# Segment 3 of a gated attention and long-convolution kernel: attention's two parts added on VectorE before the transpose, in a new order of steps

## The chip, the core and the metric

The kernel runs on one core of a Trainium2 chip. The metric is the device time of one execution in microseconds; lower is better. TensorE (PE; its weight loads are shown apart as PEld), VectorE (DVE), ScalarE (ACT), GpSimd (POOL) and SyncE (SP) run their own instruction streams in order and wait for each other by semaphores. DMAs are issued from the queues of SP and ACT here.

## What is computed

Two branches read the same x, 2048 rows of 512, and a gate mixes them by row:

```python
g = sigmoid((x * gate_w).sum(-1, keepdims=True))
out = g * A(x) + (1 - g) * B(x)
```

A is attention with 32 heads of 16 in four segments of 512 rows, with a memory M, z of the segments before. Per head and segment:

```python
logits = qs @ ks.T * scale + mask
a_dot = softmax(logits) @ vs
pq = phi(qs)                      # phi(t) = t + 1 if t > 0 else exp(t)
a_mem = (pq @ M) / (pq @ z + 1e-6)
o = sig(beta) * a_mem + (1 - sig(beta)) * a_dot
M, z = M + phi(ks).T @ vs, z + phi(ks).sum(0)
```

The o of all heads side by side are multiplied by wo. B is a long convolution of x with a kernel made from state-space parameters; the program does it with two levels of transforms written as matmuls, and adds a skip term.

## The kernel before

The program is recorded first and replayed after. `build_graph` makes a list of 1678 steps; each step names its engine, a function that issues its instructions, and the tiles that it reads and writes. `ORDER` is a table of numbers, made ahead of time: each entry is a step's number, then, after a slash, the buffer that each new tile takes; a letter a or v says whether ACT or DVE does a step that either can do. `replay` (line 233) walks the table, and `emit` (line 262) gives each engine its steps in that order, with the waits that the data and the reuse of buffers need. So the order on every engine and on every DMA queue, the choice of engine for copies out of PSUM, and the buffers all come from this table.

Almost every matmul is issued by one helper, so PE's rows read line 707. `evac` (line 222) copies a PSUM tile to SBUF: line 224 on ACT or 225 on DVE, lines 227 and 228 with a scale.

Attention. Heads are taken in four groups of eight (hg 0 to 3) per segment s. `project` makes q and k, `scores` does five score tiles per group: PE writes the scores into banks 0 to 3 of PSUM, ACT makes their exponential (line 1182, eighty in all), DVE masks them (line 1195), and PE multiplies them with v (the 17-column matmuls). `norm` divides by the sums (lines 1146, 1147, 1149) into `o1`, a bf16 tile of 128x512. `ophase` (line 1212) reads the memory for s > 0 (136-column matmuls; lines 1229, 1232 and 1233 on DVE) into `o2`, also bf16 128x512. It then brings both into the transposed form that the product with wo needs, as `oT`:

```python
        srcs = [o1] + ([o2] if o2 is not None and s < SUMO else [])
        one = len(srcs) == 1
        P3 = S.ps(dt=BF16 if one else F32)

        def f3(e):
            for tb in range(4):
                if one:
                    i = e.transpose(ap(P3, tb * 128, n=128), ap(o1, tb * 128, n=128), ap(ident, n=128))
                    continue
                for si, T in enumerate(srcs):
                    i = mm(e, ap(P3, tb * 128, n=128), ap(T, tb * 128, n=128), ap(ident, n=128), si == 0 and tb == 0, si == len(srcs) - 1)
```

With `SUMO = 4` no segment has the sum made on DVE (line 1237): in segments 1 to 3 PE multiplies o1 and o2 with the identity, eight matmuls of 128 columns that add up in a float32 PSUM tile. Segment 0 has no o2 and transposes o1 alone (four, line 1247).

The convolution. `ssm_prep`, `ssm_powers`, `ssm_cb` and `tables` make the transform of its kernel, mostly on DVE (lines 802 to 884 and 1286 to 1306). `x_level1` transforms x and writes it to scr_Z in HBM. `tail` runs twice (halves a and b): spectra (lines 1424 to 1433), products (1458), inverse transforms (1477).

The end. `early` multiplies the oT of segments 0 and 1 with wo (512-column matmuls, four to a tile) and puts the results back over oT. `finals` does the last level of the convolution (256-column matmuls with 32 rows of output, 16 to a tile) and adds attention: for segments 0 and 1 on DVE (line 1532), for 2 and 3 by more 512-column matmuls into the same PSUM tile, followed by the gate's scale (lines 227, 228, 1536, 1537). Segment 3's last tiles take three of their four head groups first and the fourth, hg 3, last. Output rows go out by DMA from SP and ACT.

The first loads: the identity comes by ACT's queue; the log of dt, x, the parameters, `c_W` (the first transform) and the weights by SP's.

Of the kernel before, what the change touches and what calls it, by code (L numbers as in the profile page):

```python
# [366 lines left out]
SUMO = 4  # L367
# [9 lines left out]
192/0 10/0 9/1 206/1 388/0 215/0 15/0 0/0 59/1 12/2 22/0 16/0 7/0 1210/0 27/3 3/0 28/0 17/0 20/0 25/1 33/0 13/1 26  # L377
42/12 23/0 60/7 35/0 43/1 34/6 36/2 1/0 41/11 62/4 37/3 38 39 1189/1 40 48/0 44/3 50/4 61v/0 14/4 49/5 1221/1 51/13
11/5 53/6 1211/0 63a 45 52 46 64/0 66/0 1213/4 47 1212a/0 1223/5 65 67v/4 76/0 211/2 78/5 1214a 79v/0 77 55/2 1215
90/2 88/2 19/0 91v/6 207/6 56/4 89 18/0 1224v/1 100/2 373/0 102/5 54/13 195/3 101 212a 103v/7 112/0 58/0 29/5 80 104  # L380
114/1 1197/7 31/0 113 81 57 1195/4 1190/2 92 188/0 68 1222a 30v/0 124/3 126/3 1225 209/1 189 1196a/0 181/4 69 1198a
1205/5 32v/1 213/4 208a 115v/1 1199 125 210a 1207/7 93 201/0 72/2 70/0 176/7 5/0 136/1 204/1 139v/2 105 138/6 202a/2
137 214a 1192/0 116 140 196/0 205a/0 127v/3 141 389/3 177/2 1206a/1 203/1 1208a 178/0 148/1 184/3 1218/1 223/0
151a/5 224 1191v/0 390a 150/5 293/2 225/1 149 965v/0 179/2 1193a 163v/8 226/0 182/1 227 197/0 294a/0 1194 383/0 185
1209 228/2 190 117 252/3 969/1 966v 164 128 180 129 384v/1 160/2 230/0 216 231 198 253a/1 71 1216/2 199/0 374/0
191/0 232/0 970 165 255/3 967v 162/9 579/0 971/0 84/7 972/0 1219a/0 295/2 238/0 375 968v 239 1217a 973 229/0 391/1
240/1 254/0 24 152 974/1 1228/2 217 233 200/0 977/0 1220 256a/2 975 242/0 234 392a 183 976 376 1229a/1 243 986/1
1226/1 244/0 1252/0 218/2 235/0 380/3 161 2/0 985 978 987 381a/2 264/0 219/0 979 265 1227a 241/3 220/0 245 988 266/0
1230 246 980/1 153 1202/1 82/3 981 271/0 4/0 272 1203a/0 172 247/2 989/1 173 273/1 395/1 83 236 983/0 94/1 248 982
267/0 268 396a 269/2 237/0 1200/1 296/2 990 1231/1 984 580/0 1201a 279/0 581 992/1 280 297a/0 1204 1265/1 270/0  # L390
281/0 274 382/1 275 186 96/3 1263/2 276/3 997 1264a/1 249 283/0 277 284 1266a 998/0 278/1 285/1 1267 999 257/1
1255/3 221 784/0 377 1001/0 222/2 1000 282/0 991 258/0 310/0 1256a/0 311 259/0 312/2 260 286 287 95 378 993 332/1
1253/3 106/3 288/0 303/0 1002 304 333a/1 107/1 994 305/0 1234/1 1235a/1 289 1003 306/0 290 307 1254a 1232/1 193 261
308/1 1257 995/1 298/3 250/0 1027/0 1233a 194 318/0 319 299/0 1236 262/0 309/1 320/0 313 301 335/2 300/0 108 996 314
118/1 322/0 120/6 323 336a/2 1004/1 324/1 315/4 1005 119 1010/3 316 1011 1012 263/0 1237/2 317/0 130/3 334/0 1014/4
1025/1 73v/7 1015 1238a/1 1006/7 132/4 1007 1016a/0 187 1008 582 74 1013a 785/5 1028/0 1023a/0 1247/1 1239/2 1026
1249/3 1009a 1021v 786 1024v 251a/0 1022v 344/0 1032 1248a/0 345 1033/0 1030/1 321/0 1240a 346/1 1034 1241 1244/2
1029 393/1 1250a 85v/0 1031 351/0 109a/4 1251 352 1036/0 325 394a 1035 353/2 440/1 1041 1242/3 1042/1 110 326 111
441a/0 86 347/0 1037 87 1243a/1 348 437/1 1043 349/1 1017/0 1038 327/2 1045/0 438a/0 363/0 1047 1245a 364 350/1
365/0 354 1246 337/3 328 1044 75 302/2 1039/1 355 338/0 397 359/0 1046 97a/1 360 329 1019 1053 361/1 485/0 339/0  # L400
1054/0 1040 291/3 292a 404/0 1055 121a/6 405 98 1057/1 340 486a/1 1056 341 406/0 1048/0 1270/0 1268/3 1271a/1 407/0
1058 408 1269a 342 1059 409/2 362/2 1272 1060/1 1260/0 1258/3 1049 366 367 99 1061 1259a/0 593/1 411/0 1020 1018
1051/0 412 1261a 413/1 1262 596/0 1050 600/3 122 1052 133a/2 399/4 601a 134 597a 131 1070/6 135 1062/7 356/1 400/0
# [1237 lines left out]
```

## Time and profile before

| | us |
|---|---|
| three runs | 282.5, 282.64, 284.19 (median 282.64) |
| the profiled execution | 282.45 |
| its span, first to last instruction | 280.6 |
| PE busy | 247.3 |
| DVE busy | 261.4 |
| ACT busy | 251.1 |

The span is what the trace shows of the profiled execution; the rest of its time lies around it. In the profile's groups a line gives the number of instructions, their busy time in all, the mean of one in ns, and the engine's idle time before them. Since an engine starts an instruction while the one before it drains, the busy time of a group is less than the count times the mean. In the chain and the timeline a row gives the start, the length, the engine and the line.

### The profile page before, as it was taken

The numbers are of one execution on the slowest core, as the hardware profiler recorded it, in microseconds if no ns is written. First come the engines' busy times: TensorE is split into PE (matmuls) and PEld (weight loads), VectorE is DVE, ScalarE is ACT, GpSimd is POOL, SyncE is SP. The second block draws the span as 40 slices with busy tenths as digits, with TensorE's granted clock in tenths as the row PEclk, the third lists the DMA queues.
The fourth block names the chain that finished last, engine by engine and source line by source line (L and its number), as shares of the span: only waits on it lengthen the run. The fifth ranks groups of instructions, "written<-read, shape, count | busy, mean of one in ns | idle before, by whom it ended". The sixth has DMA issues, their size and how long they took to land.

```text
span 280.6 us, 11488 instructions
## 1 busy us (share of the span) xinstructions
PE 247.3 (88%) x5042; PEld 160.0 (57%) x5042; DVE 261.4 (93%) x641; ACT 251.1 (89%) x310; POOL 5.1 (2%) x11
## 2 busy tenths in 40 slices
PE   2677887878978899999999998899999999999994
PEld 1342354645555766677666576566477656656672
DVE  0999999999999999999999999999999999998772
ACT  3999999999999999999999999999999998987621
POOL 5000000000000000000000000000000000000000
PEclk9999999999999999999999999999999999999999
DMA  7895493621232545334632646677577775330136
GB/s 171 261 247 139 126 221 98 183 65 41 88 89 61 160 111 174 116 94 105 223 103 70 176 134 199 198 216 245 160 248 195 232 210 154 86 97 5 40 92 172
DMA packets 47427, 40.70 MB, mean 145 GB/s; under 512 B 21265, under 2 KB 44818, under 8 KB 47378
## 3 DMA queue, kind: packets, MB, share of 16 engines
q1 hardware_dynamic: 46226, 39.43, 49.6%
q8 instruction: 39, 0.64, 1.0%
q10 hardware_dynamic: 1152, 0.56, 0.8%
q14 instruction: 10, 0.08, 0.1%
HBM read 20.64 MB, written 6.29 MB: 96 GB/s over the span
## 4 chain that ended last, share of the span: by engine, by line
PE 40%; ACT 35%; DVE 17%; issue 5%; DMA 1%; ACTq 0%
PE psum L707 40%; ACT sb L1182 19%; ACT sb L224 11%; DVE sb L225 3%; ACT sb L840 1%; DVE sb L1432 1%; DVE sb L848 1%; DVE sb L1195 1%; DMA sb<-c_ident 1%; DVE sb L847 1%; ACT sb L855 1%; DVE sb L1458 1%; DVE sb L856 1%; ACT sb L1022 1%; DVE sb L1292 1%
## 5 line engine op out<-in xcount | busy, mean ns | idle before, releaser
L707 PE MATMUL psum<-sb 128*64 128x17 bf16 (+16 forms) x4938 | 240.8, 222 | 24.2 <-ACT sb L1182 11.1
L707 PEld LDWEIGHTS psum<-sb 128*64 128x64 bf16 (+8 forms) x4938 | 153.5, 102 | 108.3 <-ACT sb L1182 23.7
L1182 ACT ACTIVATE sb<-psum 128x2048 bf16<-128x2048 f32 (+1 forms) x80 | 138.1, 1726 | 9.9 <-PE psum L707 9.2
L224 ACT ACTIVATE sb<-psum 128x512 bf16<-128x512 f32 (+6 forms) x151 | 91.7, 660 | 3.4 <-PE psum L707 3.0
L1289 DVE TENSOR_TENSOR sb<-sb 128x512 bf16<-128x512 bf16 (+2 forms) x44 | 30.5, 702 | 0.0
L1286 DVE TENSOR_TENSOR sb<-sb 128x512 bf16<-128x512 bf16 (+2 forms) x44 | 30.5, 701 | 0.0
L1292 DVE TENSOR_TENSOR sb<-sb 128x512 bf16<-128x512 bf16 (+2 forms) x44 | 30.3, 703 | 0.0
L1458 DVE TENSOR_TENSOR sb<-sb 128x1024 bf16<-128x1024 bf16 x32 | 21.1, 678 | 0.0
L225 DVE CAST sb<-psum 128x512 bf16<-128x512 f32 (+1 forms) x28 | 19.4, 702 | 0.5 <-PE psum L707 0.3
L1195 DVE TENSOR_TENSOR sb<-sb 128x512 bf16<-128x512 bf16 (+1 forms) x40 | 18.3, 468 | 0.0
L1432 DVE TENSOR_TENSOR sb<-psum,sb 128x512 bf16<-128x512 f32 x26 | 16.9, 680 | 0.5 <-ACT sb L224 0.4
L1149 DVE TENSOR_TENSOR sb<-psum,sb 128x256 bf16<-128x256 f32 x32 | 13.3, 415 | 0.2
L840 ACT ACTIVATE sb<-sb 128x512 f32<-128x512 f32 x18 | 11.7, 649 | 1.1 <-DVE sb L847 0.8
L1146 DVE RECIPROCAL sb<-psum 128x16 f32<-128x16 f32 x32 | 7.9, 247 | 1.1 <-PE psum L707 1.1
L1233 DVE TENSOR_TENSOR sb<-psum,sb 128x512 bf16<-128x512 f32 x12 | 8.2, 687 | 0.2
L1079 ACT ACTIVATE sb<-sb 128x512 bf16<-128x512 bf16 x12 | 7.6, 634 | 0.0
L1022 ACT ACTIVATE sb<-psum 128x512 bf16<-128x512 bf16 x12 | 7.4, 620 | 0.2 <-PE psum L1019 0.2
L848 DVE SCALAR_TENSOR_TENSOR sb<-sb 128x256 f32<-128x256 f32 (+1 forms) x18 | 7.4, 414 | 0.0
L847 DVE TENSOR_TENSOR sb<-sb 128x256 f32<-128x256 f32 (+1 forms) x18 | 7.4, 413 | 0.0
L1532 DVE SCALAR_TENSOR_TENSOR sb<-psum,sb 128x512 bf16<-128x512 f32 x8 | 5.9, 733 | 1.6 <-PE psum L707 1.6
L225 DVE COPY sb<-psum 128x512 f32<-128x512 f32 (+1 forms) x8 | 6.7, 837 | 0.2
L776 DVE COPY sb<-psum 128x512 bf16<-128x512 bf16 x1 | 0.7, 724 | 6.5 <-PE psum L773 6.5
(87 smaller groups left out, 123.2 us busy)
## 6 DMA issues: line engine op xcount, KB each, us to landing
sb<-c_DNM SPq DMA_DIRECT2D x16, 640.0 KB, 4.5
sb<-sb SPq DMA_DIRECT2D x64, 128.0 KB, 3.2
scr_Z<-sb SPq DMA_DIRECT2D x16, 256.0 KB, 2.5
sb<-scr_Z SPq DMA_DIRECT2D x32, 128.0 KB, 3.5
sb<-in_A_x_dram SPq DMA_DIRECT2D x5, 512.0 KB, 5.2
sb<-sb SPq DMA_DIRECT2D x20, 64.0 KB, 2.1
out_dram<-sb SPq DMA_DIRECT2D x18, 64.0 KB, 1.7
sb<-sb SPq DMA_DIRECT2D x8, 136.0 KB, 3.7
```

Source lines behind the costliest of these rows:

```text
L224: fa = lambda e: e.activation(dst(), src(), ACT.Copy)
L225: fd = lambda e: e.tensor_copy(dst(), src())
L707: mm = lambda e, o_, l, r_, st, sp, **kw: e.matmul(o_, lhsT=l, rhs=r_, start=st, stop=sp, skip_group_check=True, **kw)
L840: op("ACT", ("As", 512), lambda e, sq=sq, Z=Z: e.activation(ap(sq, n=512), ap(Z, n=512), ACT.Square), r=[Z], w=[sq], key=PW[h] + PWS * k)
L1149: op("DVE", ("V1", 256), lambda e: e.tensor_tensor(ap(o1, gi * 16, [[128, 4], [32, 4], [1, 16]]), ap(T, dims=[[68, 4], [17, 4], [1, 16]]), ...
L1182: o = op("ACT", ("Ax", 4 * w), lambda e, P=P, pT=pT, w=w: e.activation(ap(pT, dims=[[w, 4], [1, w]]), ap(P, dims=[[512, 4], [1, w]]), ACT. ...
L1195: op("DVE", ("V2", 1024 if ent is None else 512), lambda e, pT=pT, pd=pd, md=md: e.tensor_tensor(ap(pT, dims=pd), ap(pT, dims=pd), md(), A ...
L1286: op("DVE", ("V2" if n > 1 else "V1", 256 * n), lambda e: e.tensor_tensor(run(tile, ne, dst, 1), sa(), ap(pw, cl * 512, [[2, 128], [0, n], ...
L1289: op("DVE", ("V2" if n > 1 else "V1", 256 * n), lambda e: e.tensor_tensor(run(t2, n, 0, 1), sa(), ap(pw, cl * 512 + 256, [[2, 128], [0, n] ...
L1292: op("DVE", ("V2" if n > 1 else "V1", 256 * n), lambda e: e.tensor_tensor(D_(), D_(), ap(t2, n * 128, [[-n * 128, 2], [2 * n, 64], [1, 2 * ...
L1432: op("DVE", ("V1", 512), lambda e, Ks=Ks, PE_=PE_, Os=Os, sg=sg, al=al: e.tensor_tensor(ap(Ks, 512 * sg, n=512), ap(PE_, n=512), ap(Os, n= ...
L1458: op("DVE", ("V2", 1024), lambda e, Y=Y, X=X, K3=K3: e.tensor_tensor(ap(Y, dims=[[512, 2], [256, 2], [1, 256]]), ap(X, dims=[[256, 2], [0, ...
```

## The change

`SUMO` goes from 4 to 3. In segment 3, and there alone, DVE adds o2 to o1 in place (line 1237: one bf16 add of 128x512 for each of the four head groups), and PE transposes the sum into a bf16 PSUM tile: four transposes (line 1247) in place of eight accumulating matmuls. The program has 1682 steps, and `ORDER` is another table throughout: other places, other buffers, and other engines for some of the copies.

```diff
-SUMO = 4
+SUMO = 3
...
 ORDER = """
-192/0 10/0 9/1 206/1 388/0 215/0 15/0 0/0 59/1 12/2 22/0 16/0 7/0 1210/0 27/3 3/0 28/0 17/0 20/0 25/1 33/0 13/1 26
...
+16/0 215/0 10/5 9/3 0/0 15/0 59/0 1214/1 388/0 192/0 7/0 206/1 12/4 27/5 11/2 17/7 20/0 28/0 25/1 33/0 26 14/5 35/3
...
```

What differs in the two programs, by count of instructions:

| engine | form | before | after |
|---|---|---|---|
| PE | 128-column matmuls, line 707 | 224 | 192 |
| PE | transposes, line 1247 | 16 | 32 |
| DVE | adds of line 1237 | 0 | 4 |
| ACT, DVE | 512 wide out of PSUM (lines 224, 225) | 123, 32 | 129, 26 |
| ACT, DVE | 1024 wide out of PSUM | 16, 4 | 15, 5 |
| ACT, DVE | 256 wide within SBUF (lines 224, 225) | 5, 11 | 9, 7 |
| ACT, DVE | scaled, 512 wide (lines 227, 228) | 2, 5 | 5, 2 |

The eighty exponentials stand in the same sequence in both. Ahead of some of them, this many instructions stand on each engine (before, after):

| ahead of exponential | PE matmuls | ACT | DVE |
|---|---|---|---|
| 1 | 136, 117 | 37, 33 | 59, 52 |
| 34 | 1975, 1975 | 162, 163 | 303, 301 |
| 66 | 3960, 3960 | 270, 272 | 532, 529 |
| 75 | 4474, 4466 | 293, 297 | 595, 590 |
| 80 | 4802, 4826 | 301, 310 | 623, 620 |

Three places of the new order. The first is the last head group of segment 3, on PE; the fence has PE before the change, from the product of segment 2 with wo that follows the last scores. The 128x128 rows are oT of groups 2 and 3, the 128x17 and 64x17 rows the last probabilities times v, the 128x512 rows products with wo:

```order
L707 MATMUL psum<-sb 128x512 x4
L707 MATMUL psum<-sb 32x256 x80
L707 MATMUL psum<-sb 128x136 x4
L707 MATMUL psum<-sb 128x512 x4
L707 MATMUL psum<-sb 128x128 x8
L707 MATMUL psum<-sb 128x17 x24
L707 MATMUL psum<-sb 64x17 x32
L707 MATMUL psum<-sb 128x512 x6
L707 MATMUL psum<-sb 128x128 x8
L707 MATMUL psum<-sb 32x256 x32
```

And PE after the change at the same place:

```order
L707 MATMUL psum<-sb 128x512 x4
L707 MATMUL psum<-sb 128x136 x4
L707 MATMUL psum<-sb 32x256 x48
L1247 MATMUL psum<-sb 128x128 x4
L707 MATMUL psum<-sb 128x17 x24
L707 MATMUL psum<-sb 64x17 x32
L707 MATMUL psum<-sb 128x512 x10
L1247 MATMUL psum<-sb 128x128 x4
L707 MATMUL psum<-sb 32x256 x32
```

Between the last 64x17 row and the last oT stand ten 512-column matmuls where six stood, and each oT has four transposes of line 1247.

The same place on DVE, before, from the mask of the last probabilities (line 1195) on; lines 1146 to 1149 are the last normalisation, line 225 copies the last oT:

```order
L1195 TENSOR_TENSOR sb<-sb 128x4x2x64
L1229 SCALAR_TENSOR_TENSOR sb<-psum,sb 128x32
L1232 RECIPROCAL sb<-sb 128x32
L1532 SCALAR_TENSOR_TENSOR sb<-psum,sb 128x512
L1233 TENSOR_TENSOR sb<-psum,sb 128x512
L1146 RECIPROCAL sb<-psum 128x16
L1147 TENSOR_TENSOR sb<-sb 128x16
L1149 TENSOR_TENSOR sb<-psum,sb 128x16x16
L1532 SCALAR_TENSOR_TENSOR sb<-psum,sb 128x512
L225 CAST sb<-psum 128x512
```

And DVE after:

```order
L1195 TENSOR_TENSOR sb<-sb 128x4x2x64 x2
L1233 TENSOR_TENSOR sb<-psum,sb 128x512
L1146 RECIPROCAL sb<-psum 128x16
L1147 TENSOR_TENSOR sb<-sb 128x16
L1149 TENSOR_TENSOR sb<-psum,sb 128x16x16
L1237 TENSOR_TENSOR sb<-sb 128x512
L1532 SCALAR_TENSOR_TENSOR sb<-psum,sb 128x512 x2
```

The add of line 1237 stands between the last normalisation and what follows; the last oT is no longer copied by DVE, and one more output of line 1532 comes behind the add.

The second place is ACT from the 76th exponential to the 80th, before; line 1079 is an exponential of q:

```order
L1182 ACTIVATE sb<-psum 128x2048
L1079 ACTIVATE sb<-sb 128x512
L1182 ACTIVATE sb<-psum 128x1024
L1182 ACTIVATE sb<-psum 128x2048 x3
L227 ACTIVATE sb<-psum,sb 128x512
```

And ACT after, from the 76th exponential on; line 975 is an exponential of the gate:

```order
L1182 ACTIVATE sb<-psum 128x2048
L224 ACTIVATE sb<-psum 128x4x128
L975 ACTIVATE sb<-psum 128x16
L1182 ACTIVATE sb<-psum 128x1024
L227 ACTIVATE sb<-psum,sb 128x512
L1079 ACTIVATE sb<-sb 128x512
L227 ACTIVATE sb<-psum,sb 128x512
L1182 ACTIVATE sb<-psum 128x2048
L227 ACTIVATE sb<-psum,sb 128x512
L1182 ACTIVATE sb<-psum 128x2048
L224 ACTIVATE sb<-psum 128x4x128
L1182 ACTIVATE sb<-psum 128x2048
```

Three scaled outputs (line 227) and a copy of line 224 come ahead of the 80th; the other copy and line 975 stood ahead of the 76th before, where a new copy of line 224 stands now.

The third place is the start of SP's queue, before, from its third load (x for attention) on; the names are the tensors:

```order
L220 DMA sb<-in_A_x_dram 128x4x512
L220 DMA sb<-in_B_B_im_dram 128x4x128
L220 DMA sb<-in_gate_w_dram 128x4x1
L220 DMA sb<-c_W 128x256
L220 DMA sb<-in_A_x_dram 128x2048
L220 DMA sb<-c_negm 128x128
L220 DMA sb<-in_A_wv_dram 128x4x512
L220 DMA sb<-in_B_C_re_dram 128x4x128
L220 DMA sb<-in_A_beta_dram 128x32
L220 DMA sb<-c_mk 128x1
```

And after, from the same load on:

```order
L220 DMA sb<-in_A_x_dram 128x4x512
L220 DMA sb<-in_A_x_dram 128x2048
L220 DMA sb<-c_W 128x256
L220 DMA sb<-in_B_B_im_dram 128x4x128
L220 DMA sb<-in_B_B_re_dram 128x4x128
L220 DMA sb<-in_A_wv_dram 128x4x512
L220 DMA sb<-in_B_C_im_dram 128x4x128
L220 DMA sb<-in_A_wk_dram 128x4x512
L220 DMA sb<-in_B_C_re_dram 128x4x128
L220 DMA sb<-in_A_x_dram 128x2048
```

The 128x2048 load of x, which the first transform of the convolution reads, moved from the seventh place to the fourth, wk came forward to the tenth, and gate_w, negm, beta and mk moved back.

More of the change, by code (lines that the diff above doesn't have):

```diff
@@ L382 @@
[L382 to L391, printed above, removed]
@@ new lines @@
+1233a/1 1230/2 982 244/1 978/1 1256/1 391/3 5/0 237/1 983 784/0 172 392a 977 264/0 1231a 265 984/0 241/3 376 266/1
+979 218/1 1206/2 245 985 381a/2 271/0 990/1 219/0 272 1234 395/0 989 273/2 220/0 246 991 1204/1 95/0 1235/0 1207a/0
+987/0 267/0 173 268 1205a 269/0 247/0 1208 580/1 96 296/2 993/1 221 992 986 396a 279/0 280 297a/1 270/0 581 377
+108/6 281/1 274 1267/2 995 275 1269/1 248 994 1268a/1 276/1 283/0 996/1 284 1270a 222/2 285/0 1271 277 249 278/0
+1259/3 997 257/1 785/0 258/0 310/0 1260a/0 786 311 1001 332/0 1002/1 312/2 988 282/3 286 387/0 1003 106/1 259/0
@@ new lines @@
+489a/0 424 1277/0 1089 166/3 1279/3/2 425/0 1090/0 1094 167 1091 494/0 1096/1 452/0 1280a/0 1102/0 453 1281a 426
+495/0 454/1 1283/3 1289/2 1101 1285/3 427 1095 1282/0 1290a/2 459/0 1103 1286a/1 1302/1 460 534/2 428/5 461/0 1306/0
+1097 531/0 1104 1105/0 174 371/3 429 1098 175 583 582 498/0 372a 499 385/0 458/3 1106 500/0 462 1291/1 463 430
+535a/2 467/0 1287/0 532a/2 468 1108/0 1303/2 469/0 1292/0 1324/1 1114/1 1113 1314/0 1107 1293a/0 471/0 472 1304a/1
+1115 1294/0 1297/0/1 1109 473/1 1295 1116 464/1 1117/0 1099/1 470/2 1298a/0 474 1299a 501/0 1118 502 1100 1301/2
@@ new lines @@
+1136 518 510/5 1150 519/2 1328/1 511 492/0 1152/1 1145 543 1351/0 1151 1329a/0 549/0 544 550 1153 516/0 551/0
+1333/2/3 512/0 491 1147 1155/1 1340/1 1334a/0 546/0 1341a/1 547 1336/0 520 548/1 1344/1 1335 521 1345a/2 1158/0
+1338/1 553/0 554 1157 552/2 1337/2 555/1 588/1 522/5 1159 1358/0 642/3 587/2 1381/1 523 1160 1134 1161/0 589a/1
+561/0 524 1330 562 1154 525/0 563/2 1331 556 557 526/0 1133 1162 527 558/2 1170/0 643a/1 609/0 528/1 610/0 483/3
+1342/0 1359/1 1346/1 1362/0 1360a/0 565/0 566 559 484a 1169 1352/1/0 560/1 567/0 1171 1156 1347/1 1172 1353a/0
@@ new lines @@
+710/0 708 1457/0 1447/1/3 711/1 1384/1 1395/1 681/1 682 683 736/0 1437/0 1448a/0 712 722/0 737a/1 1449/0 1385/1
+723/2 1450 709/0 738/1 1452/2 713 1386v/0 714 1451/3 718/0 1441/1 1408/1 636/1 719/0 739/1 637/1 638 639/0 715/0
+1458/2 724 647/0 1473/3 1510/0 1459v/3 1442/2 740a/0 1394/0 716 649 1474a/5 1456/3 1397/2 1484/1 1443a/0 684/3
+1460/2 698/3 1415/0 640/1 699/0 685/3 720 1461/2 1398a/1 700/0 695/0 686 696/0 1466/3/2 701 1462a/1 687/1 717/0
+641a/0 1463/0 758/0 697 721/0 1467v/0 759/1 21/0 725 843/1 1469/1 1468 1477/2 844a/2 656/0 1471/0 751/0 1478v/3 726
@@ new lines @@
+1536/2 1542/1/0 1520 840 783v 1521 889a/1 860 851/0 1532/3 852/0 1423/1 849/0 856 1543a/0 1580/1 1537/2 853 1424a/0
+868 1584/0 857/0 1544/1 1538a/1 1425 861 862 1545 848/0 870/0 1547/0 863/1 1588/1 841/2 871/1 864 1561/3/1 850
+1546/1 865/0 842v/0 1593/0 1562a/0 872 900/0 1563/0 869/2 901/2 873 1564 1553/1 874 1594v 1565/2 1549/3 1554v/4
+1572/0 1566/3 1550a/3 893/0 875/4 1585 1540 927/1 891/0 894/1 876 877 1539 1555/1 1568/3 1573a/5 878/2 1426 1551/3
+928a/0 1599/7 1569a/2 879/5 880 1556/0 1600a 881/0 890/0 895 896/0 1557a/0 1582 1597/3 1570/3 897/0 1574/0 1559
```

131 lines of the change are left out of this document (58 added, 73 removed).

## The prediction

> **What bounds the kernel now.** I read the span and clock first, then the busy shares, then the busy time by stage, and last the chain of work that ended last. The span and the page's busy line, and the stages cut at exponentials of attention (line 1182, which run in one sequence of eighty):
>
> ```profile
> core 0: 280.6 us, clock 1.000
> PE 247.3 (88%) x5042; PEld 160.0 (57%) x5042; DVE 261.4 (93%) x641; ACT 251.1 (89%) x310; POOL 5.1 (2%) x11
> 0.00:27.40 27.40, 17.05 (x132) 8.06 (x132) 20.74 (x58) 21.38 (x41) 3.82 (x9) 1.00 0.79 209
> 27.40:126.00 98.60, 85.78 (x1836) 55.10 (x1837) 98.24 (x246) 97.27 (x127) 0.66 (x1) 1.00 0.42 116
> 126.00:224.50 98.50, 93.00 (x2006) 63.68 (x2001) 96.36 (x230) 94.36 (x110) 0.66 (x1) 1.00 0.60 179
> 224.50:250.70 26.20, 25.31 (x516) 16.39 (x513) 25.67 (x64) 23.61 (x25) 0.00 (x0) 1.00 0.49 142
> 250.70:264.50 13.80, 13.74 (x329) 8.87 (x330) 12.11 (x30) 9.69 (x8) 0.00 (x0) 1.00 0.09 23
> 264.50:281.00 16.50, 12.45 (x244) 7.88 (x243) 8.30 (x19) 4.81 (x6) 0.00 (x0) 1.00 0.47 119
> ```
>
> The columns are the stage, its length, then busy time with the count of instructions for PE, PEld, DVE and ACT. The clock is full throughout. No engine bounds the whole: from the 1st to the 34th exponential (27.4 to 126) DVE and ACT are full, DVE with 0.36 us idle of 98.6 and ACT with 1.3, while PE has 12.8 idle. Up to the 66th (224.5) all three are 94 to 98% busy. Then it turns: from 250.7 to 264.5 PE has 0.06 us idle, DVE 1.7 and ACT 4.1. The chain that ended last says the same of the end:
>
> ```profile
> 231.31 0.48 PE psum L707 x32
> ...
> 232.99 17.63 PE psum L707 x355
> 250.63 3.87 PE psum L707 x44
> ...
> 256.66 20.31 PE psum L707 x440
> 276.99 0.69 ACT sb L227
> ```
>
> From 232.99 to 276.99 it is PE for 17.63 + 3.87 + 20.31 = 41.8 of 44.0 us. So a PE instruction saved in the last segment is worth its issue time; DVE or ACT work added there is free while it fits their idle time; and work added in the first 126 us on DVE or ACT would be paid in full.
>
> **The change part by part.** The prices:
>
> ```profile
> L707 PE MATMUL psum<-sb 128*128 128x128 bf16 x224 | 20.1, 220 | 0.0
> 82.71 0.39 PE L1247 MATMUL psum<-sb 128*128 128x128 bf16 x4
> L707 PE MATMUL psum<-sb 128*128 128x512 bf16 x288 | 75.4, 388 | 7.5 <-ACT sb L224 3.9 <-DVE sb L225 1.5 <-DVE sb L808 1.1
> L1082 DVE TENSOR_TENSOR sb<-sb 128x512 bf16<-128x512 bf16 x8 | 3.2, 403 | 0.0
> L224 ACT ACTIVATE sb<-psum 128x512 bf16<-128x512 f32 x111 | 64.6, 623 | 3.1 <-PE psum L707 2.8
> L224 ACT ACTIVATE sb<-psum 128x1024 bf16<-128x1024 f32 x15 | 15.3, 1036 | 0.3 <-PE psum L707 0.2
> L224 ACT ACTIVATE sb<-sb 128x256 bf16<-128x256 bf16 x5 | 2.4, 483 | 0.0
> L227 ACT ACTIVATE sb<-psum,sb 128x512 bf16<-128x512 f32 x2 | 1.4, 687 | 2.5 <-PE psum L707 2.5
> L225 DVE CAST sb<-psum 128x512 bf16<-128x512 f32 x27 | 18.2, 682 | 0.5 <-PE psum L707 0.3
> L225 DVE CAST sb<-psum 128x1024 bf16<-128x1024 f32 x1 | 1.2, 1225 | 0.0
> L225 DVE COPY sb<-psum 128x512 f32<-128x512 f32 x5 | 3.4, 688 | 0.2
> L225 DVE COPY sb<-sb 128x256 bf16<-128x256 bf16 x11 | 2.9, 291 | 0.0
> L228 DVE TENSOR_SCALAR sb<-psum,sb 128x512 bf16<-128x512 f32 x5 | 3.7, 730 | 2.4 <-PE psum L707 2.4
> ```
>
> *PE.* Each of the four head groups of segment 3 had 8 accumulating 128-column matmuls and has 4 transposes now: 16 fewer. A 128-column matmul lasts 220 ns, but four in a row take 0.39 us (the row at 82.71), so each further one adds (0.39 - 0.22) / 3 = 0.057 us. The ends are 0 (if PE waits there for something else) and the average busy time, 16 x 20.1 / 224 = 1.4. I take 16 x 0.057 = 0.9 us, since in a full queue the spacing counts. That row is four transposes of segment 0 (line 1247), so I price transposes and matmuls alike. The Trainium skill says otherwise ("TensorE: Matmul & The Clock Gate", Part 4: PE-mode transpose): about 275 ns for a 128x128 transpose within a kernel, and that transposes don't count as activity for the clock gate. By that figure 16 transposes would be 4.4 us in place of 32 x 0.057 = 1.8, and the sum 285.0 (an estimate) instead of the one below; the row at 82.71 disagrees, with four in 0.39 us at full clock.
>
> *The adds.* DVE gets four bf16 adds of 128x512. The nearest row is line 1082, the same shape and types: 403 ns, 1.6 us in all. By their place among the exponentials one stands before the 69th, where DVE has 0.5 us idle in the stage, two after the 77th and 78th (1.7 idle), and one after the 80th (8.2 idle). Only the last lies between the last normalisation and the last transpose:
>
> ```profile
> 270.80 0.26 DVE L1146 RECIPROCAL sb<-psum 128x16 f32<-128x16 f32 x1 [0.74 <-PE psum L707]
> 271.10 0.17 DVE L1147 TENSOR_TENSOR sb<-sb 128x16 f32<-128x16 f32 x1
> 271.31 0.42 DVE L1149 TENSOR_TENSOR sb<-psum,sb 128x256 bf16<-128x256 f32 x1
> ...
> 272.42 2.08 ACTq L220 DMA_DIRECT2D out_dram<-sb  x4
> ...
> 274.55 0.47 ACT L1536 ACTIVATE sb<-psum,sb 128x256 bf16<-128x256 f32 x1 [4.32 <-PE psum L707]
> ```
>
> That path of DVE ends at 271.73, 0.93 us after it starts, and becomes 0.93 + 0.40 = 1.3 us. PE's cover behind the last probability matmuls was six 512-column matmuls and is ten now, 10 x 75.4 / 288 = 2.6 us. So the add costs nothing; with the old cover of 1.6 us it would also fit, and with none it would cost 0.4. Its range is 0 to 0.4. Queued behind it on DVE are the two segment-1 outputs (line 1532), which only stores wait for. ACT issued four of these stores in 2.08 us (the row at 272.42) ahead of line 1536; now two of them, 1.04 us, stand behind it, where ACT is idle from 275.02 to 276.99. That costs nothing either.
>
> *Evacuations change engine.* By the counts of the two programs ACT gets six more 512-wide (6 x 0.58), three scaled ones (3 x 0.69) and four small copies (4 x 0.48), and loses one 1024-wide (1.02): +6.5 us, from which two single instructions more are to be taken off. DVE loses six 512-wide copies (0.67 to 0.68 each), four small ones (0.26) and three scaled ones (0.73), and gains two 1024-wide casts (1.22) and the adds: -3.2 us; three single ones that nearly cancel are left out. ACT stands at 270 instructions before the 66th exponential and 272 now, at 301 and 310 before the 80th. The five between the 75th and the 80th are two 512-wide and three scaled ones, 2 x 0.58 + 3 x 0.69 = 3.2 us, against 4.1 us idle there. I take 0; the ends are 0 and +1.5 (first rival).
>
> *The new order.* The eighty exponentials keep their sequence, and ahead of the 34th, 45th, 55th and 66th stand the same number of matmuls in both programs (1975, 2840, 3333, 3960); DVE has 303 and 301 instructions ahead of the 34th, 532 and 529 ahead of the 66th. What is permuted lies within a few microseconds of its place. I take 0 for it. The gain it could bring is bounded by DVE's idle time from 27.4 to 250.7, 0.36 + 2.14 + 0.53 = 3.0 us; the loss by a like amount, taken as an estimate.
>
> *The first loads.* The order moves the second quarter of x (512 KB) from the seventh place on SP's queue to the fourth, right behind the first load of x, and wk ahead of the first write of scr_Z:
>
> ```profile
> 1.25 0.59 ACTq L220 DMA_DIRECT2D sb<-c_ident  x1
> 1.69 0.41 SPq L220 DMA_DIRECT2D sb<-in_A_x_dram  x1
> 3.78 0.43 SPq L220 DMA_DIRECT2D sb<-in_A_x_dram  x1
> 4.74 0.34 PEld L773 LDWEIGHTS psum<-sb 128*128 128x128 bf16 x4 [4.74 <-DMA sb<-c_ident]
> 6.52 0.72 DVE L776 COPY sb<-psum 128x512 bf16<-128x512 bf16 x1 [6.52 <-PE psum L773]
> ```
>
> PE's first instruction waits for the identity until 4.74, and DVE's first runs at 6.52; DVE then has 27.4 - 20.74 - 6.52 = 0.1 us idle in that stage. So nothing that arrives earlier can help by more than that, and an identity delayed by the whole of the moved load would cost 512 KB / 209 GB/s = 2.5 us. The identity, issued on ACT's queue at 1.25, was 2.5 us ahead of the moved load (3.78), and would be 0.85 us ahead of it in the fourth place, which begins when x's issue ends (1.69 + 0.41). I take 0: the identity still goes first, and the load of x right behind it (1.69) was in the same place already. Ends -0.1 and +2.5.
>
> *Sum.* The profiled execution took 282.45 us for a span of 280.6, so 1.85 lies around it. 282.45 - 0.9 + 0 + 0 + 0 + 0 = 281.55, told as 281.6. The median of the three runs is 282.64, 0.2 above the profiled execution, so this is 0.4% less than the median.
>
> **The rivals.**
> 1. *ACT paces the last exponentials* (slower than before). Between the 75th and 80th ACT would be busy 9.69 + 3.2 = 12.9 us of 13.8, and each exponential may also wait for its scores, which PE can only write once the exponential before has read the banks: 0.48 us in the chain's row at 231.31. Five of these give 12.9 + 2.4 = 15.3, 1.5 over the stage; PE, in order, then waits at the scores. That is 282.45 - 0.9 + 1.5 = 283.1. It is slower than before once over 0.9 us of it remains. For it: without those waits ACT would have only 0.9 us of slack. Against: a copy that stands between two exponentials runs while the scores are written and so hides them; and PE has 24 more matmuls ahead of the 80th (4826 against 4802) to run meanwhile.
> 2. *The first loads delay the identity.* 281.55 + 2.5 = 284.1. For it: PE and DVE both start on it. Against: the identity's issue on ACT's queue does not change.
> 3. *PE is not the limit of the last segment*, and the saved matmuls turn into waiting: 282.5. The rows speak against it by 0.06 us of idle time. The Trainium skill supports it ("Perfetto Trace Analysis", Identifying the Most-Contended Engine): matmul busy time is no measure of PE's limit, weight-load time is, and that is 8.87 us of 13.8 in this stage.
> 4. *Transposes are dearer than matmuls*: if each took its 220 ns in full, 16 x 0.22 = 3.5 us would replace 1.8, so 282.45 + 1.7 = 284.2. Against it stands the row at 82.71. (This is the way of the Trainium skill's Part 4, cited above.)
> 5. *The new order closes waits in the middle.* With all of DVE's 3.0 us of idle time gone: 281.55 - 3.0 = 278.6; with two thirds, 279.6. For it: all three engines have some idle time between 126 and 224.5. Against: the counts ahead of each exponential are unchanged there.
>
> **How the numbers follow.** Forecast 0.46 (281.6, its own spread 280.3 to 282.9); rival 1 0.15, rival 2 0.11, rival 3 0.09, rival 4 0.04, rival 5 0.15. The range runs from rival 5's middle to just over rivals 2 and 4: 279.0 to 284.6, which leaves about one in ten at each side. One per cent, 2.8 us, is about what a measurement of this kernel can tell from no change. Faster by more than that (under 279.8) is rival 5 and a little of the forecast's lower end: 0.18. Slower by more (over 285.5) needs two of rivals 1, 2 and 4 together, or a loss in the middle as large as the gain of rival 5: 0.10. Within 1%: 0.72.
>
> **What would show it.** PE's sum falls by about 1.4 us and DVE's by about 3, ACT's rises by 5 to 6.5. Line 1237 shows four adds near 403 ns, line 1247 has 32 matmuls, four in 0.39 us. The 34th and 66th exponentials start within 1 us of 126.0 and 224.5 (rivals 2 and 5 fall), the first DVE instruction within 0.3 us of 6.52 (rival 2 falls), PE still has under 0.5 us idle between the 75th and 80th (rivals 1 and 3 fall), and the chain again ends in one long PE piece. The prediction is wrong if the 34th exponential comes over 2 us late or early, for then the new order, which I price at nothing, decides the time.

## The result, and the profile after

The changed kernel took 282.05 us (median of 18 runs, 280.64 to 283.35), the kernel before 283.67 in the runs beside them (18 runs, 282.0 to 285.71). The ratio is 0.995, 95% interval 0.9929 to 0.9971: half a per cent faster, which stands clear of zero and lies within the 1% that was called no change. A second set of runs gave 282.16 against 283.36, 0.9948 (0.9921 to 0.9976). The forecast was 281.6 with 279.0 to 284.6, and no change as the likeliest. The number held, but two of the terms behind it did not, and the medians of both kernels hold something that the profile of before did not show: windows at half clock.

The span and clock of the profiled execution (282.41 us), and its busy line:

```profile
core 0: 280.6 us, clock 0.994
PE 241.7 (86%) x4984; PEld 160.7 (57%) x5026; DVE 258.6 (92%) x635; ACT 255.3 (91%) x320; POOL 5.1 (2%) x11
```

DVE fell by 2.8 us and ACT rose by 4.2. PE's sum isn't to be compared, since 42 of the 5026 matmuls have no record; another profile of the kernel before with as many missing has 243.3, 1.6 more. The span equals that of before, 280.6. But the clock reads 0.994, where before had 1.000.

To see past that I cut both traces at the same instructions: VectorE's first, the start of the 34th, 66th and 80th exponential, and the end of the last instruction that computes. The columns are the stage, its length, busy time with counts for PE, PEld, DVE, ACT and POOL, and the granted clock. The kernel before:

```profile
6.52:125.98 119.46, 101.07 (x1957) 62.35 (x1959) 118.96 (x303) 116.22 (x164) 0.66 (x1) 1.00 0.49 134
125.98:224.48 98.50, 93.00 (x2007) 63.68 (x2002) 96.36 (x230) 94.36 (x109) 0.66 (x1) 1.00 0.60 178
224.48:264.53 40.05, 39.10 (x844) 25.29 (x842) 37.83 (x92) 33.32 (x33) 0.00 (x0) 1.00 0.35 101
264.53:277.68 13.15, 12.42 (x244) 7.87 (x242) 8.27 (x19) 4.80 (x6) 0.00 (x0) 1.00 0.49 124
```

The changed kernel, first profile:

```profile
6.01:126.79 120.78, 99.37 (x1934) 64.10 (x1956) 120.58 (x305) 116.44 (x164) 0.00 (x0) 0.99 0.50 135
126.79:224.58 97.79, 91.35 (x1998) 63.50 (x2005) 94.53 (x225) 94.05 (x111) 1.22 (x2) 1.00 0.62 176
224.58:265.83 41.25, 38.61 (x860) 25.49 (x863) 36.21 (x91) 36.89 (x39) 0.00 (x0) 1.00 0.34 99
265.83:277.68 11.85, 10.63 (x201) 6.79 (x204) 7.29 (x17) 5.52 (x7) 0.00 (x0) 1.00 0.58 149
```

And the stretch in which its clock fell, with the same length ahead of it:

```profile
117.65:121.06 3.41, 2.51 (x82) 1.90 (x83) 3.41 (x7) 3.07 (x4) 0.00 (x0) 1.00 0.40 107
121.06:124.48 3.42, 3.42 (x24) 2.24 (x25) 3.42 (x5) 2.75 (x3) 0.00 (x0) 0.50 0.40 104
```

For 3.42 us PE runs at half clock. The first stage, 1.3 us longer than in before, holds it. A later profile of the same kernel, without such a stretch there, has:

```profile
5.83:125.09 119.26, 97.65 (x1934) 63.26 (x1956) 119.06 (x301) 116.44 (x164) 0.00 (x0) 1.00 0.50 136
125.09:223.26 98.17, 91.41 (x1998) 63.49 (x2005) 96.19 (x229) 94.12 (x110) 1.22 (x2) 1.00 0.61 178
223.26:264.47 41.21, 38.61 (x860) 25.49 (x864) 36.21 (x91) 36.93 (x40) 0.00 (x0) 1.00 0.33 92
264.47:276.31 11.84, 10.63 (x201) 6.78 (x204) 7.29 (x17) 5.52 (x7) 0.00 (x0) 1.00 0.57 149
```

So the half clock cost 120.78 - 119.26 = 1.5 us in that profile. Leaving it out, the changed kernel needs 119.26 + 97.79 + 41.21 + 11.84 = 270.10 us from VectorE's first to the last computing instruction, the kernel before 119.46 + 98.50 + 40.05 + 13.15 = 271.16: 1.1 us less. That takes the second stage from the first profile; with the later one's own 98.17 it is 0.7 less. The first stage is 0.2 shorter and the second 0.7 (0.3 with 98.17), the third 1.2 longer, the last 1.3 shorter; these two go together, since the new order has more work ahead of the 80th exponential.

The chain that ended last, in order of time (start, length, engine, what it writes, line):

```profile
260.98 1.41 DVE sb L1532 x2
262.39 0.34 DVE sb L1149
262.75 0.42 DVE sb L1237
263.18 0.67 DVE sb L1195 x2
264.08 0.42 DVE sb L1082
264.51 1.32 DVE sb L1532 x2
266.11 2.47 PE psum L707 x55
...
274.62 2.35 PE psum L707 x37
```

In before it was PE alone from 256.66 to 276.97. Now 5.1 us of it, 260.98 to 266.11, are VectorE's, one of the adds (262.75) among them. The later profile has the same pieces.

### The profile page after: what moved, and what is told of

It reads as the page before. It is cut to its first block, busy times and chain, and to the rows that moved or that the text cites. A ratio compares the mean times of both kernels' runs of the same rounds, so it can differ in the third digit from the quotient of the medians.

```text
span 280.6 us, 11417 instructions
## 1 busy us (share of the span) xinstructions
PE 241.7 (86%) x4984; PEld 160.7 (57%) x5026; DVE 258.6 (92%) x635; ACT 255.3 (91%) x320; POOL 5.1 (2%) x11
## 4 chain that ended last, share of the span: by engine, by line
DVE 40%; PE 34%; ACT 21%; issue 3%; DMA 1%; ACTq 0%
PE psum L707 33%; ACT sb L1182 15%; DVE sb L1286 5%; DVE sb L1289 5%; DVE sb L1292 5%; ACT sb L224 4%; DVE sb L225 3%; DVE sb L1432 2%; DVE sb L847 2%; DVE sb L848 2%; DVE sb L1195 1%; DVE sb L1458 1%; DVE sb L1149 1%; DVE sb L856 1%; DMA sb<-c_ident 1%
## 5 line engine op out<-in xcount | busy, mean ns | idle before, releaser
L707 PE MATMUL psum<-sb 128*64 128x17 bf16 (+18 forms) x4864 | 233.7, 221 | 28.0 <-ACT sb L1182 10.9
L707 PEld LDWEIGHTS psum<-sb 128*128 128x128 bf16 (+8 forms) x4906 | 152.4, 102 | 104.7 <-ACT sb L1182 27.7
L224 ACT ACTIVATE sb<-psum 128x512 bf16<-128x512 f32 (+5 forms) x155 | 94.2, 655 | 5.9 <-PE psum L707 4.8
L225 DVE CAST sb<-psum 128x512 bf16<-128x512 f32 (+2 forms) x27 | 19.9, 745 | 1.3 <-PE psum L707 1.1
L1019 PE MATMUL psum<-sb 128*128 128x128 bf16 x48 | 4.6, 219 | 1.6 <-ACT sb L1182 0.7
```

Of the source, the lines that this page charges most:

```text
L224: fa = lambda e: e.activation(dst(), src(), ACT.Copy)
L225: fd = lambda e: e.tensor_copy(dst(), src())
L707: mm = lambda e, o_, l, r_, st, sp, **kw: e.matmul(o_, lhsT=l, rhs=r_, start=st, stop=sp, skip_group_check=True, **kw)
```

## The experiments

The theories. *T*: the saved PE work pays 0.9 us in the last segment and the order nothing (the forecast). *O*: the new order makes the gain, by closing waits ahead of the last segment, and the half clock takes part of it back. Line numbers in the kernels below whose table was set anew can be one lower (1181 for 1182).

**1. The sum alone.** The order of before, four adds put in.

```diff
-SUMO = 4
+SUMO = 3
 ORDER = (before's)
-... 782/2 835 783a 851/0 ...
+... 782/2 835 840 783a 851/0 ...
```

(840 is the first add, 835 the last normalisation of its group; the three others alike.)

> The order of before, with only the sum in segment 3: four adds on VectorE, each right behind the last normalisation and memory step of its head group, and 16 PE matmuls fewer; no evacuation changes its engine and no load moves. Theory 1 (the forecast's step: PE is the limit of the last segment, each matmul saved is worth 0.057 us): 0.9 us under before, ratio 0.997; the first exponential starts within 0.1 us of before's 27.4, and the stretch from the 66th exponential to the end is 0.9 us shorter than before's 56.1. Rival (the saved PE work turns into waiting, as it does in the changed kernel, where this stretch is only 0.1 us shorter): 0 to 0.1 us, ratio 1.000. Without a stage at half clock, as before's profile has none: granted clock 1.000.

Measured: 283.83 against 283.34, ratio 1.0013 (0.9983 to 1.0043). The last two stages:

```profile
225.50:266.13 40.63, 37.68 (x829) 24.74 (x834) 38.50 (x94) 33.44 (x32) 0.00 (x0) 1.00 0.35 99
266.13:279.09 12.96, 11.68 (x232) 7.34 (x234) 9.07 (x21) 4.81 (x6) 0.00 (x0) 1.00 0.47 119
```

They take 53.59 us, 0.4 more than the 53.20 of before. Executions at full clock have the same span as those of before, 280.4 us (medians, the table in experiment 7). So theory T falls in this order; its rival, no gain, came nearer. Of PE's work only one weight load waits for an add here, 0.6 us. But VectorE has no idle time between 231 and 254 us, so each add pushes back what stands behind it: the products of line 1457 come 20.30 us after the 66th exponential, at 245.80, in the second profile of before (experiment 7) 19.71 after it, at 245.90. PE's matmuls wait for such steps, where they don't in either profile of before:

```profile
247.14 1.05 PE L706 MATMUL psum<-sb 64*128 64x256 bf16 x16 [0.33 <-DVE sb L1457]
...
258.26 1.70 PE L706 MATMUL psum<-sb 128*128 128x17 bf16 x64 [0.28 <-DVE sb L1194]
```

**2. The same, with the adds late.** Each add stands right ahead of its transposes.

```diff
-... 782/2 835 840 783a ... 894/0 1551/2 841/3 1569a/1 ...
+... 782/2 835 783a ... 894/0 1551/2 840 841/3 1569a/1 ...
```

> The order of before with the sum, as in the first experiment, but each add now stands right ahead of its head group's transposes instead of right behind the last normalisation and memory step. Theory P (the first experiment's tail was 0.5 us longer because the adds stood on VectorE ahead of evacuations that PE and ScalarE waited for): behind the 66th exponential 55.5 to 56.0 us instead of 56.66. Rival Q (PE is not what the tail of before waits for, whatever the place of the adds): 56.2 to 56.7.

Measured: 285.37 against 283.27, 1.0063 (1.0024 to 1.0102); the two stages take 41.16 + 14.41 = 55.57 us, 2.4 over before. Both guesses missed on the same side. PE's timeline says why, with what ended the idle time in brackets:

```profile
241.82 0.40 PE L1246 MATMUL psum<-sb 128*128 128x128 bf16 x4 [0.68 <-DVE sb L1236]
...
256.65 0.40 PE L1246 MATMUL psum<-sb 128*128 128x128 bf16 x4 [0.88 <-DVE sb L1236]
...
270.43 0.40 PE L1246 MATMUL psum<-sb 128*128 128x128 bf16 x4 [0.74 <-DVE sb L1236]
...
274.05 0.40 PE L1246 MATMUL psum<-sb 128*128 128x128 bf16 x4 [0.61 <-DVE sb L1236]
```

Each of the four groups of transposes waits for its add, 0.68 + 0.88 + 0.74 + 0.61 = 2.9 us. The add isn't the 0.4 us of its own length: it queues behind what VectorE has in front of it. Against that the same places in the changed kernel, first the two groups of instructions (count, busy time, mean ns, idle time before them), then PE and VectorE around the last head group:

```profile
L1247 PE MATMUL psum<-sb 128*128 128x128 bf16 x32 | 3.1, 220 | 0.1
L1237 DVE TENSOR_TENSOR sb<-sb 128x512 bf16<-128x512 bf16 x4 | 1.7, 422 | 0.1
```

```profile
268.52 0.40 PE L1247 MATMUL psum<-sb 128*128 128x128 bf16 x4
...
272.22 0.39 PE L1247 MATMUL psum<-sb 128*128 128x128 bf16 x4
```

```profile
271.12 0.43 DVE L1237 TENSOR_TENSOR sb<-sb 128x512 bf16<-128x512 bf16 x1
```

The last add ends at 271.55, and PE, at work on other matmuls, reaches the transposes at 272.22, which wait for nothing (no bracket). All 32 transposes together have 0.1 us of idle time ahead of them. Both profiles of the changed kernel show no instruction that waits for an add. The new order has room for it, the old one has not.

**3. The order alone.** The changed kernel's table without the adds, eight accumulating matmuls again. It ran twice.

```diff
-SUMO = 3
+SUMO = 4
 ORDER = (the changed kernel's, without the four adds)
```

> The order of the changed kernel with its loads and evacuations, but the four adds taken out and attention's dot and memory parts accumulated by eight matmuls for each head group as before. Theory 1 (the sum gives 0.9 of the changed kernel's 1.6 us, the order the rest): 0.7 us under before, ratio 0.998. Rival (the sum gives at most 0.1 in this order, the order's earlier start gives about 1.0 to 1.9 and the stage at half clock takes some back): 1.5 us under before, ratio 0.995, as the changed kernel. Both: VectorE starts at 6.0 instead of 6.5 us, and PE's granted clock falls to 0.5 for one window of 3.4 us near 121 us in most executions (mean 0.994).

> The new order without the sum (as in the second experiment), beside the changed kernel. Theory (the sum is worth 0.68 us in this order, as the two profiles show behind the 66th exponential): at full clock 0.7 us longer than the changed kernel. Rival (it is worth the forecast's 0.9, or nothing): 0.9, or 0.

Measured: 282.06 against 283.34, 0.9967 (0.9937 to 0.9996); the second time 282.5 against 283.36, 0.9979 (0.9947 to 1.001). The first profile had no window at half clock, which I had expected in most executions (10 of 24 had one):

```profile
6.52:125.71 119.19, 97.19 (x1934) 63.10 (x1956) 118.98 (x301) 116.33 (x164) 0.00 (x0) 1.00 0.50 135
125.71:223.50 97.79, 91.35 (x1999) 63.51 (x2005) 96.10 (x229) 94.06 (x111) 1.22 (x2) 1.00 0.62 177
223.50:265.16 41.66, 39.00 (x868) 26.11 (x873) 35.66 (x89) 36.96 (x39) 0.00 (x0) 1.00 0.33 96
265.16:277.27 12.11, 10.96 (x209) 7.09 (x210) 6.71 (x15) 5.41 (x7) 0.00 (x0) 1.00 0.57 146
```

Ahead of the 66th exponential it needs 216.98 us, before 217.96: 0.98 less. VectorE's idle time (length less busy time) falls from 0.50 + 2.14 to 0.21 + 1.69 = 0.74 less, its work by 0.24. Which of the new places close these waits was not found. Behind the 66th it takes 53.77, 0.57 *more* than before; both profiles of this kernel have the same 41.66 and 12.11 there. The sum brings that to 53.1 (41.25 + 11.84, 41.21 + 11.84): 0.7 us. In executions at full clock the spans say the same, 279.7 us (median of 14) and, for the changed kernel, 279.0 (of 12). So in this order the sum is worth 0.7 us, near the forecast's 0.9; PE's busy time in these two stages falls by as much, 0.39 + 0.33. Theory O is right on the order ahead of the last segment and wrong that the sum is nothing.

**4. Half of the order.** The new order up to the 66th exponential, the old one from there, no sum; and the reverse, with the sum. Buffers that were still taken at the seam were given anew, and six steps came a little later.

```diff
 ORDER =
+ (the changed kernel's steps up to the 66th exponential)
+ (what is left, as before has it)
```

> The new order (loads and evacuations with it) up to the 66th exponential, from there the order of before without the sum. Theory S (the new order is worth about 1.0 us ahead of the 66th exponential, by less VectorE waiting, and nothing behind it): executions at full clock last about 279.3 us from the first to the last instruction, 1.0 under the 280.3 of the kernel before at full clock; from VectorE's first instruction to the 66th exponential 217.0 us instead of 218.0; behind it 56.2 as before. Rival N (the front's gain is only the first load's jitter of up to 0.75 us from one execution to the next): 280.3 at full clock, 218.0 to the 66th exponential.

> The order of before up to the 66th exponential, from there the changed kernel's order with the sum. Theory S (tail and front are worth what they are worth alone): behind the 66th exponential 56.0 us as in the changed kernel, 0.15 under before; at full clock 280.15. Rival M (the new tail needs the evacuations that the new front leaves): 56.5 or more, no faster than before.

Measured: 284.19 against 283.27, 1.0015 (0.9983 to 1.0046), and 285.57, 1.0047 (1.0014 to 1.008). The first of the two:

```profile
5.86:125.05 119.19, 99.83 (x1954) 63.06 (x1956) 118.98 (x301) 116.32 (x165) 0.00 (x0) 1.00 0.51 137
125.05:222.84 97.79, 92.80 (x2010) 63.49 (x2005) 96.07 (x229) 94.02 (x110) 1.21 (x2) 1.00 0.61 175
222.84:264.99 42.15, 39.10 (x845) 25.33 (x842) 38.26 (x93) 33.33 (x33) 0.00 (x0) 1.00 0.35 100
```

The front came out as forecast, 216.98 for 217.0. But the 40.05 us behind it became 42.15: at the seam PE waits for an exponential, and the next exponential for PE's scores:

```profile
227.18 3.15 PE L706 MATMUL psum<-sb 128*128 128x512 bf16 x31 [1.00 <-ACT sb L1181]
```

```profile
229.84 1.88 ACT L1181 ACTIVATE sb<-psum 128x2048 bf16<-128x2048 f32 x1 [2.19 <-PE psum L706]
```

The reverse also loses behind the 66th (43.57 + 11.84 against 41.25 + 11.84), with a window at half clock at 230.1 in its profile. Two of its executions were at full clock, with spans of 281.4 and 281.9 us, over 2 us above the changed kernel's 279.0, so it isn't the window alone. That the old tail after the new front, or the reverse, is worth what it is worth in its own kernel was wrong; why the seam costs two microseconds, and what the new buffers and the six later steps have in it, was not followed further.

**5. The engines back.** The changed kernel's order, with the 56 evacuations and copies that had changed their engine on before's.

```diff
-67a/4 ... 1216v/1 ... 30a/1 ... 1228a/0 210v ...
+67v/4 ... 1216a/1 ... 30v/1 ... 1228v/0 210a ...
```

> The changed kernel's order and sum, but each of the 56 evacuations and copies that changed its engine is back on the engine that the kernel before gave it. Theory E (the front's 0.98 us came mostly from the order: VectorE's waits fell by 0.74 us, its work by 0.24): from VectorE's first instruction to the 66th exponential 217.2 us instead of 217.0 (before: 218.0), behind it within 0.5 us of the changed kernel's 53.1 us up to the last computing instruction. Rival F (the order is cut to these engines, and without them the waits come back): 218 us or more to the 66th exponential, and 1 us or more behind it.

Measured: 294.56 against 283.36, ratio 1.0402 (1.0358 to 1.0445). Theory E had expected a fraction of a microsecond; rival F was right, by far more than its 218. The two stages of the front:

```profile
5.89:129.00 123.11, 97.60 (x1929) 63.27 (x1951) 119.03 (x301) 117.00 (x165) 0.00 (x0) 1.00 0.49 133
129.00:229.14 100.14, 91.94 (x2003) 63.71 (x2008) 95.96 (x231) 94.32 (x109) 1.21 (x2) 1.00 0.60 173
```

VectorE has no more to do (119.03 and 95.96 against 119.06 and 96.19), yet the stages are 3.9 and 2.0 us longer: its idle time rose to 123.11 - 119.03 = 4.1 and 4.2 us. Behind the 66th exponential it loses another 5.6 (45.40 + 13.23, with a window at half clock in it). This order is cut to the engines that it was made for.

**6. The load back.** The second quarter of x at the seventh place of SP's queue again.

```diff
-10/5 ... 15/0 59/0 1214/1 ... 7/0 ... 12/4 ... 11/2 ...
+10/5 ... 15/0 59/0 ... 7/0 ... 12/4 ... 11/2 1214/1 ...
```

> The changed kernel with the second quarter of x back at the seventh place of SP's queue. Theory (the prediction's step: the place of this load is worth nothing, since neither the identity nor VectorE's first instruction waits for it): from the identity's arrival to VectorE's first instruction 1.78 us as in all kernels so far, to the 34th exponential 119.2 us after VectorE's first instruction, as without a half-clock window. Rival (the early place pays for the first exponential's earlier start, 19.5 us after VectorE's first instruction instead of 20.85, and that is kept): 0.3 to 1.3 us more to the 34th exponential.

Measured: 281.37 against 283.36, 0.9948 (0.9923 to 0.9973); the changed kernel beside it 282.16. The first stage:

```profile
5.70:124.94 119.24, 97.69 (x1934) 63.23 (x1956) 119.03 (x301) 116.42 (x164) 0.00 (x0) 1.00 0.51 138
```

119.24 us, as with the load in its early place (119.26). The place is worth nothing. That the median is lower is the clock's doing: 8 of its 12 executions were at full clock, 6 of 12 of the changed kernel's beside it, with spans of 279.35 and 279.1 us in the middle.

**7. The half clock.** Once more the kernel before, and the changed kernel; and two with extra work for PE (matmuls issued again into the same PSUM tile), meant to keep it active where it waits or moves little.

```diff
+FILL, FILLAT = 6, ((0, 5),)
...
-                for c in range(2):
+                for c in [0, 1] * (FILL if (half, t) in FILLAT else 1):
                     for pi in range(2):
```

The second of these has `FILL = {(0, 5): 6, (0, 8): 2, (0, 10): 2, (1, 1): 2, (1, 2): 2}`, the repeats for each half and step.

> The kernel before, unchanged, for more executions with their granted clock. Theory A (the half clock is a matter of the new order's PE activity near 120 us): clock 1.000 in all executions, ratio 1.000. Rival (a window at half clock comes in before too, in some executions): some with 0.994, those about 1 to 1.5 us longer than the others.

> The changed kernel, unchanged, beside the next one. Executions at full clock last 278.9 to 279.4 us from the first to the last instruction, those with one window at half clock 1.4 more; from VectorE's first instruction to the last computing one 270.1 without such a window.

> The changed kernel with the second half-step of one inverse-transform's matmuls of segment 1 (at about 120 us, ahead of the stage at half clock) issued six times over into the same PSUM tile, where PE would else wait 0.9 us for ScalarE's exponential; the result is the same, only PE does more. Theory A (the half clock at 121.06 to 124.48 us follows from PE's low activity in the window before, and costs the changed kernel 1.4 us): granted clock 1.000 in the profile and nearly all executions, 280.7 us, 1.4 under the changed kernel, ratio to before 0.990. Rival B (the half clock has another cause, say the long run of PE work before): it stays at 0.994 and the time at 282.0 or above by the added 0.5 us of matmuls, ratio 0.995 to 0.997. Rival C (the half clock costs nothing, since VectorE bounds there): clock 1.000 and the time stays within 0.3 us of the changed kernel's.

> The changed kernel with more PE work at five places of low activity (the inverse transform's second half-step issued six times at about 119.7 us, and twice at about 149, 172 and, two of them, 182.5 us; the result is the same). Theory A (a window of 3.4 us at half clock follows a window in which PE moves little through the full array): at most 3 of 12 executions below a granted clock of 0.997 instead of 12 of 18, median 281.1, 0.9 under the changed kernel's 282.05. Rival B (it comes at other places as often): half of the executions or more at 0.994 or below, median 282 or above. In both: up to 0.4 us longer at full clock than the changed kernel's 278.9.

The kernel before, beside itself, gave 283.44 against 283.34 (1.001, 0.998 to 1.0039). It has such windows too; this profile has two. Each pair is the window ahead and the one at half clock:

```profile
47.41:50.83 3.42, 2.63 (x89) 2.25 (x93) 3.42 (x9) 3.42 (x5) 0.00 (x0) 1.00 0.73 226
50.83:54.24 3.41, 3.41 (x45) 2.35 (x45) 3.41 (x11) 3.15 (x5) 0.00 (x0) 0.50 0.47 121
180.53:183.95 3.42, 2.97 (x79) 1.94 (x82) 3.02 (x8) 3.06 (x3) 0.00 (x0) 1.00 0.52 137
183.95:187.36 3.41, 3.19 (x20) 1.97 (x20) 2.15 (x7) 2.37 (x2) 0.00 (x0) 0.50 0.81 215
```

By the clock and the span that each execution leaves (0.997 or more is full clock, or a window that lies behind the last computing instruction, as in the later profile of the changed kernel, where it starts at 277.61; the executions in neither group show other values, most of them 0.988 or less, as two windows give):

| kernel | executions | at full clock | median span, time of these | at 0.993 or 0.994 | median span |
|---|---|---|---|---|---|
| before | 111 | 54 | 280.4, 282.41 | 35 | 282.0 |
| changed | 30 | 12 | 279.0, 280.80 | 17 | 280.6 |
| order alone | 24 | 14 | 279.7, 281.88 | 7 | 281.5 |
| sum alone | 12 | 4 | 280.4, 282.19 | 7 | 282.3 |

At full clock the changed kernel is 1.4 us shorter by span and 1.6 by time. Of before's executions 57 of 111 lie below 0.997, of the changed kernel's 18 of 30, so it is no matter of the new order, and the expectation that before stays at 1.000 fell. Filling did not shorten the kernel: with one place filled 283.12 against 283.34 (0.9994, 0.9969 to 1.002), 8 of 12 executions still below 0.997 (this time overstates the cost: it lies 2.7 us over the span, where the other kernels have 1.8 or 1.9, and the span at full clock is 279.65, the median of four); with five places 283.41 against 283.27 (1.0003, 0.997 to 1.0036), 5 of 12 below, but 281.4 us at full clock, 2.4 longer. The forecast of at most 3 of 12 and 0.4 us was wrong twice. Whether the one filled place did its part isn't shown: the profile's window is now at 183.75, 18.4 windows of 3.41 us behind 121.06, so the windows begin elsewhere there. No version here was clearly faster than the changed kernel.

## Why the prediction came out

**PE, -0.9.** The mechanism was right only together with the new order: 0.7 us there. The step that failed is "a PE instruction saved in the last segment is worth its issue time". In the old order it was worth nothing (+0.4 with the adds early, +2.4 late): PE waits for the add itself where it stands late, and for the steps of VectorE that it pushes back where it stands early. PE's long runs in the chain were true of before; the change itself puts VectorE's steps into them, as the chain after shows, and the sign that it would again end in one long PE piece failed. Rival 3, saved matmuls that turn into waiting, holds for the old order and not for the new one.

**The adds, 0.** 422 ns each against 403 taken. No instruction waits for their results in the new order, though one of them lies in VectorE's stretch of the chain. In the old order the 0 was wrong: "free while it fits their idle time" counts the idle time of a whole stage (0.5 us from the 66th to the 75th exponential), and VectorE has none between 231 and 254 us, where two of the early adds stand. The range of 0 to 0.4 came from the add's own length; what PE waited for it without cover was its place in VectorE's queue, 0.61 to 0.88 us.

**The evacuations, 0.** ACT rose by 4.2 us where 5 to 6.5 were forecast; the two single instructions that the text left to be taken off, and shorter means (619 ns for 623), are part of it. Rival 1, ScalarE pacing the last exponentials, fell: between the 75th and the 80th ScalarE itself idles, 1.95 us for PE's scores ahead of the exponential at 260.43, and what PE waits for longest is VectorE:

```profile
251.28 6.38 PE L707 MATMUL psum<-sb 128*128 128x512 bf16 x127 [0.40 <-DVE sb L1146]
...
262.01 3.76 PE L707 MATMUL psum<-sb 128*128 128x512 bf16 x107 [0.21 <-DVE sb L1532]
```

The sign of under 0.5 us of idle PE there doesn't hold, though (0.9, and 0.6 in the second profile of before, which like it lacks records and so shows too much). To price the engines apart from the order was the mistake: moved back alone they cost over 11 us.

**The new order, 0.** This is the term that was wrong: -0.98 us ahead of the 66th exponential (-0.5 by the changed kernel's later profile, with its 98.17) and +0.57 behind it, -0.4 in all; by the spans at full clock it is -0.7 (279.7 against 280.4). It is rival 5's mechanism (VectorE's waits), at a third of its bound of 3.0. The argument against it, equal counts of instructions ahead of the 34th and 66th exponential, says nothing on waits: 0.3 and 0.45 us of them went, and no count changed by more than three.

**The first loads, 0.** Right, by experiment 6. The identity came earlier, not later (at 4.22 us; before 4.74), but so it did in the second profile of before (3.99). That is the spread of executions, and VectorE's first instruction follows 1.78 or 1.79 us behind in all of them. The sign "within 0.3 us of 6.52" failed (6.01), but with such a spread it says nothing on the change. Rival 2 fell.

**Transposes as dear as matmuls.** Right: 219 ns each by their median, four in 0.39 to 0.40 us (268.52, 272.22). Rival 4 fell, and with it the price of the Trainium skill ("TensorE: Matmul & The Clock Gate", Part 4) of 275 ns each.

**The sum.** -0.7 and -0.4 make -1.1 against the forecast's -0.9: too near for its terms, since one error covered the other: that is luck. So is the nearness of 281.6 to the median. The profile of before had full clock by chance, as half of the executions have; its 282.45 is the time at full clock (282.41), and the change at full clock gives 280.80, 1.6 less where 0.9 was forecast. The medians lie above both since they mix in the other half. Between 0.3 and 0.7 us of the 1.4 that the spans show at full clock isn't found in the stages of the few profiles; the spread of the first load's arrival is larger than that.

## What to carry to other kernels

In this kernel a saving on the engine that the chain names paid only where the step that replaces it had cover: look at what the replacement queues behind and at what it pushes back, not at its own length. An order and the engines that it was made for belonged together here, and couldn't be undone by parts. Where gains of half a per cent are weighed, sort the executions by granted clock first, and cut the traces at the same instructions.

## What was not expected of the hardware

PE falls to half clock for one window of 3.41 us though it isn't idle: in the window ahead it was busy 2.51 of 3.41 us with 82 matmuls, 2.63 with 89, and 2.97 with 79 (the rows above). The Trainium skill ("TensorE: Matmul & The Clock Gate", Part 1) has the free-running window of 3413 ns, which agrees, and one idle window as the cause, which these rows don't bear out. The starts lie on a grid: 183.95 - 50.83 = 133.12 us, 39 windows of 3.413. Where the grid falls differs from one execution to the next: the windows of the changed kernel's two profiles, at 121.06 and 277.61, lie 45.9 windows apart. That may be why the same kernel has one at 50.83 and 183.95, or none. A window cost 1.5 us at 121.06, 0.5 at 50.83 (the first stage takes 120.00 us there, 119.46 without), and at 183.95 what this stage of the kernel before has over its 98.50:

```profile
125.78:226.19 100.41, 93.06 (x1995) 64.37 (x2002) 96.42 (x230) 94.38 (x109) 0.66 (x1) 0.98 0.61 173
```

100.41 - 98.50 = 1.9 us.

Of the 82 matmuls in the window ahead of 121.06, 56 have 17 columns, and the windows ahead of 50.83 and 183.95 hold as many of them. But it isn't these matmuls alone: ahead of 230.12 in the second kernel of experiment 4 PE was busy for half of the window, with 20 matmuls, none of 17 columns:

```profile
226.71:230.12 3.41, 1.64 (x20) 0.72 (x18) 3.34 (x11) 2.62 (x3) 0.00 (x0) 1.00 0.80 188
```

What these windows share is little data through the array. Count for each matmul its columns times the share of the array's rows and columns in use (a few matmuls have no record): in the fourteen profiles all ten windows at half clock ahead of the last computing instruction follow one of the 37 windows with the smallest sums, of over a thousand. The other 27 of the 37 were followed by full clock. So little data goes with it, and from which amount, or what else it takes, was not settled.
